# A sparse attention and FFN kernel: the first batch's steps in a written order on all engines, with the first two weight conversions between them

## Chip, core and metric

The kernel runs on one core of one Trainium2 chip. The metric is the device time of one execution in microseconds (us).

## The reference

For each of 8 batches and 8 heads (S = 576 tokens, D = 64) attention runs under a mask: heads 0 to 3 see the last 32 tokens, heads 4 to 7 see earlier tokens of the same class modulo 32. The heads of a token, side by side, are a row of 512 numbers, and 4608 such rows go through a feed-forward layer with 2048 inner units.

```python
scores = scale * np.matmul(q, k.transpose(0, 1, 3, 2))
...
mask_local = (rel >= 0) & (rel < stride)
mask_strided = (rel >= 0) & (pos[None, :] % stride == pos[:, None] % stride)
...
attn = np.exp(scores)
attn = attn / (np.sum(attn, axis=-1, keepdims=True) + 1e-09)
...
h = x @ w_in
g = np.where(pos, h, np.where(neg, 0.0, (h + beta) ** 2 / (4.0 * beta)))
return (g @ w_out).astype(np.float32)
```

## The kernel before

**Engines.** PE multiplies, DVE is VectorE, ACT ScalarE, POOL GpSimd; loads go out on SP's queue. A scheduler places the instructions of all engines but PE by priority; those that pass `tc.keep_in_program_order` keep the order in which they are written. PE's order is the program's.

**Weights.** `w_in` and `w_out` come as 64-bit numbers, cut into 16 pieces `f` of 128 inner units. `load_w` (L141) brings both parts of a piece into a tile `raw_f` of 1 MB; `convert_w` (L160) turns it into `w_f`, a high and a low half in `fp32r`. For each of the two parts (`i` = 0 is `w_in`, 1 is `w_out`): two scalings on ACT (L168, L170), an and/or on DVE (L171), a shift on DVE (L173), an addition on POOL (L174), then the cast to the high half on ACT (L178) and the subtraction that leaves the low half on DVE (L179). `prepare(n)` (L189) converts up to piece `n`, `stage(n)` (L183) issues loads.

**Attention of a batch** (L232) has four units `u`, 0 and 1 for the local heads, 2 and 3 for the strided ones. `score` (L237) multiplies q and k into PSUM, takes the minimum with the mask (DVE, L267), the maximum (L268), subtracts it (POOL, L269), exponentiates (ACT, L270), sums (L271 to L273) and normalises (L275). `flip` (L278) transposes on PE (tile `tp`) and copies to `pT` on ACT (L287); there are two `pT` buffers. `value` (L290) multiplies with `v` into `xp` and splits the result into a high half `xTh` (ACT, L314) and a low half `xTl` (DVE, L315). PSUM has three places "o", two "h" and three "a".

**FFN.** Tokens go in chunks, the first of 512. For each chunk `c` and piece `f`, `up(c, f)` (L332) does 12 matmuls, on three products of halves, and the nonlinearity: `u` on ACT (L345, L346), `h` on DVE (L347), `gh` on ACT (L348), `gl` on DVE (L349). `down` (L352) follows two pieces later. During chunk 0 the second batch's attention is placed between the pieces by `GROUPS` (L386).

**The start** (L368 to L382) is what the change rewrites: the loads of the first batch, then its steps in an order of names, with `prepare(1)` after the second flip and `prepare(3)` behind all:

```python
for g in ("s0", "s1", "s2", "s3", "f0", "f1", "v0", "v1", "f2", "f3", "v2", "v3"):
    first[g]()
    if g == "s3":
        stage(6)
    if g == "f1":
        prepare(1)
```

Of the kernel before, what the change touches and what calls it, by code (L numbers as in the profile page):

```python
# [16 lines left out]
P = 128  # L17
# [6 lines left out]
def tile_sparse_attention_then_ffn(  # L24
# [115 lines left out]

    def load_w(f):  # L141
        at = waits_in(f)
        held.add(at)
        if at < NF:
            raw = place(at, [P, 2, DM, 2], U32, f"raw_{f}")
            raws[f] = [(i, raw[:, i], slice(0, DM)) for i in range(2)]
            tc.keep_in_program_order(nc.sync.dma_start(raw, w_v[f]))

    def pieces(f):
# [4 lines left out]
        for i in range(2):  # L154
            for e in (slice(0, n), slice(n, DM)):
                r = o_p.tile([P, n, 2], U32, tag="ob", name=f"raw_{f}_{i}_{e.start}")
                tc.keep_in_program_order(nc.sync.dma_start(r, w_v[f][:, i, e]))
                yield i, r, e

    def convert_w(f):  # L160

        held.discard(waits_in(f))
        sums = []
        for i, raw, e in pieces(f):
            L, H_ = raw[:, :, 0], raw[:, :, 1]
            t = H_.bitcast(F32)

            tc.keep_in_program_order(nc.scalar.activation(t, t, AF.Copy, scale=2.0 ** -112))  # L168

            tc.keep_in_program_order(nc.scalar.activation(L, L, AF.Copy, scale=2.0 ** -29))  # L170
            tc.keep_in_program_order(nc.vector.scalar_tensor_tensor(  # L171
                out=L, in0=H_, scalar=0x80000000, in1=L, op0=ALU.bitwise_and, op1=ALU.bitwise_or))
            nc.vector.tensor_scalar(out=H_, in0=H_, scalar1=3, scalar2=None, op0=ALU.logical_shift_left)  # L173
            nc.gpsimd.tensor_tensor(out=H_, in0=H_, in1=L, op=ALU.add)  # L174
            sums.append((i, t, e))
        wt[f] = w = place(f, [P, 2, 2, DM], F32R, f"w_{f}")
        for i, t, e in sums:
            nc.scalar.copy(w[:, 0, i, e], t)  # L178
            nc.vector.tensor_tensor(out=w[:, 1, i, e], in0=t, in1=w[:, 0, i, e].bitcast(F32), op=ALU.subtract)  # L179
# [9 lines left out]
    def prepare(n):  # L189
        nonlocal ready  # L190
        while ready < min(NF, n):
            convert_w(ready)
# [6 lines left out]
    def load_qk(b, p):  # L199
# [6 lines left out]
        if b < 2:  # L206
            tc.keep_in_program_order(load)
        loaded[b, p, "qk"] = t

    def load_v(b, p):  # L210
# [3 lines left out]
        if b < 2:  # L214
            tc.keep_in_program_order(load)
# [16 lines left out]
    def attention(b, kinds):  # L232
# [4 lines left out]
        def score(u):  # L237
# [4 lines left out]
            for s in range(n):  # L242
                for p in range(2):
                    for i in range(I):
# [14 lines left out]
            st = st_p.tile([P, 3, 2 * SLOTS * 2], F32, tag="st", name=f"st_{b}_{u}")[:, :, :N]  # L259
# [17 lines left out]

        def flip(u):  # L278
# [3 lines left out]
            for j in range(2):  # L282
# [4 lines left out]
                nc.scalar.copy(pT[:, j, :n], tp)  # L287
            flipped[u] = pT

        def value(u):  # L290
# [6 lines left out]
            for n, R in enumerate(rows):  # L297
# [7 lines left out]
                at += R  # L305
            for p in range(2):
# [7 lines left out]
                nc.scalar.copy(dst[0], src)  # L314
                nc.vector.tensor_tensor(out=dst[1], in0=src, in1=dst[0].bitcast(F32), op=ALU.subtract)  # L315

        return {
            "s0": lambda: score(0),
            "s1": lambda: (score(1), fetch_qk(b, 2)),
            "s2": lambda: score(2),  # L320
            "s3": lambda: (score(3), fetch_qk(b + 1, 0)),
            "f0": lambda: flip(0), "f1": lambda: flip(1), "f2": lambda: flip(2), "f3": lambda: flip(3),
            "v0": lambda: value(0),
            "v1": lambda: (value(1), fetch_v(b + 1, 0)),
            "v2": lambda: value(2),
            "v3": lambda: (value(3), fetch_v(b + 1, 1)),
        }
# [133 lines left out]
```

## Time and profile before

| | us |
|---|---|
| median of 3 runs | 949.81 (949.51 to 950.14) |
| the profiled execution | 950.17 |
| its span, first to last instruction | 948.4 |
| PE busy (8112 matmul records) | 913.5 (96%) |
| weight loads on PE | 802.6 (85%) |
| DVE / ACT / POOL busy | 398.9 / 444.5 / 129.7 |

The profiled execution's own time is 1.8 us over its span. Most matmuls here leave two records in the trace. Busy time of PE counts a matmul at the clock that it had. In the text `x0` stands for the split of unit 0's values (two casts, two subtractions), `f0` for its transposes, `v0` for its value matmuls, and so on.

### The profile page before, as it was taken

To read this page: it belongs to the slowest core of one execution; us is meant where nothing else is said; L and a number is where in the kernel's file an instruction comes from. 1 tells how busy PE (TensorE), PEld (TensorE's weight loads), DVE (VectorE), ACT (ScalarE), POOL (GpSimd) and SP (SyncE) were. 2 spreads that over 40 slices of the span, in tenths; PEclk is the share of its full clock that TensorE was granted. 3 is DMA by queue.
4 is the path that set the end of the run, shared out by engine and by line. 5 is a ranking of instruction groups with operands and counts; after the bars stand their busy time and mean duration, and the time that the engine had idled before them with its cause. 6 is when DMAs were issued, how large, how long until landed. Compare 5 with 4: busy or idle time off the path is not lost.

```text
span 948.4 us, 18897 instructions
## 1 busy us (share of the span) xinstructions
PE 913.5 (96%) x8112; PEld 802.6 (85%) x8112; DVE 398.9 (42%) x744; ACT 444.5 (47%) x875; POOL 129.7 (14%) x135
## 2 busy tenths in 40 slices
PE   4768999999999999999999999999999999999998
PEld 3556788998888889888888888988888888998997
DVE  5798883224445332225434432224343533222221
ACT  3667885334455444434444344334443544433433
POOL 5255430002203100002102100001110210000000
PEclk9979999999999999999999999999999999999999
DMA  9812601002302300002202111002020200000000
GB/s 374 358 80 94 262 32 56 1 1 87 102 33 76 101 32 34 1 1 87 102 31 87 50 53 65 1 1 84 4 101 32 87 1 1 34 1 1 34 1 34
DMA packets 14915, 61.95 MB, mean 65 GB/s; under 512 B 1648, under 2 KB 1648, under 8 KB 11888
## 3 DMA queue, kind: packets, MB, share of 16 engines
q1 hardware_dynamic: 14832, 60.76, 17.7%
q8 instruction: 63, 1.03, 0.5%
q14 instruction: 20, 0.16, 0.1%
HBM read 51.31 MB, written 9.44 MB: 64 GB/s over the span
## 4 chain that ended last, share of the span: by engine, by line
PE 89%; DVE 5%; ACT 3%; POOL 2%; issue 1%; DMA 0%; SPq 0%; POOLq 0%; DVEq 0%
PE o L358 42%; PE h L338 40%; PE xp L303 3%; PE sc L251 2%; PE tp L286 2%; DVE raw L171 1%; POOL raw L174 1%; POOL pr L269 1%; DVE w L179 1%; DVE raw L173 1%; ACT raw L170 1%; ACT raw L168 1%; DVE st L271 0%; ACT pr L270 0%; DMA qk<-in_qk_l 0%
## 5 line engine op out<-in xcount | busy, mean ns | idle before, releaser
L338 PE MATMUL h<-xTh,w 128*128 128x384 f32 (+2 forms) x1536 | 424.8, 339 | 9.4 <-ACT w L178 6.2
L358 PE MATMUL o<-w,gh 128*128 128x512 f32 x1152 | 370.7, 403 | 0.0
L338 PEld LDWEIGHTS h<-xTh,w 128*128 128x128 f32 x1536 | 281.4, 189 | 25.1 <-ACT w L178 6.5
L347 DVE SCALAR_TENSOR_TENSOR h<-h,u 128x384 f32<-128x384 f32 (+2 forms) x192 | 108.5, 565 | 400.8 <-ACT u L346 400.7
L338 PE MATMUL h<-xTl,w 128*128 128x384 f32 (+2 forms) x768 | 260.3, 339 | 0.0
L345 ACT ACTIVATE u<-h,half 128x384 f32<-128x384 f32 (+2 forms) x192 | 111.4, 580 | 309.2 <-PE h L338 306.9
L358 PEld LDWEIGHTS o<-w,gh 128*128 128x128 f32 x1152 | 209.3, 189 | 39.7
L358 PE MATMUL o<-w,gl 128*128 128x512 f32 x576 | 228.7, 397 | 0.0
L338 PEld LDWEIGHTS h<-xTl,w 128*128 128x128 f32 x768 | 145.2, 189 | 10.2
L349 DVE TENSOR_TENSOR gl<-h,gh 128x384 fp32r<-128x384 f32 (+2 forms) x192 | 106.3, 553 | 73.5 <-ACT gh L348 73.3
L348 ACT CAST gh<-h 128x384 fp32r<-128x384 f32 (+2 forms) x192 | 92.6, 482 | 91.6 <-DVE h L347 91.2
L358 PEld LDWEIGHTS o<-w,gl 128*128 128x128 f32 x576 | 108.6, 189 | 26.1
L269 POOL TENSOR_TENSOR pr<-pr,st 128x648 f32<-128x648 f32 (+2 forms) x32 | 41.4, 1296 | 517.3 <-DVE st L268 490.2
L346 ACT ACTIVATE u<-u 128x384 f32<-128x384 f32 (+2 forms) x192 | 101.0, 526 | 5.0
L270 ACT ACTIVATE pr<-pr 128x648 f32<-128x648 f32 (+2 forms) x32 | 23.7, 741 | 63.8 <-POOL pr L269 63.8
L174 POOL TENSOR_TENSOR raw<-raw 128x512 uint32<-128x512 uint32 (+1 forms) x34 | 41.3, 1214 | 61.4 <-DVE raw L173 50.7
L271 DVE TENSOR_REDUCE st<-pr 128x12 f32<-128x648 f32 (+2 forms) x32 | 26.3, 821 | 47.3 <-ACT pr L270 47.3
L275 POOL TENSOR_TENSOR pr<-pr,st 128x648 f32<-128x648 f32 (+2 forms) x30 | 39.7, 1324 | 42.0 <-DVE st L273 41.3
L303 PEld LDWEIGHTS xp<-pT,v 64*64 64x64 f32 (+2 forms) x1856 | 32.6, 143 | 15.1 <-issue 7.7
L303 PE MATMUL xp<-pT,v 64*64 64x32 f32 (+2 forms) x1856 | 36.5, 228 | 7.1 <-DVE xTl L315 4.6
L251 PEld LDWEIGHTS sc<-qk 64*32 64x32 f32 (+1 forms) x2048 | 28.1, 123 | 15.5 <-issue 8.0
L251 PE MATMUL sc<-qk 64*32 64x64 f32 (+1 forms) x2048 | 33.2, 234 | 7.6 <-DMA qk<-in_qk_l 5.3
(33 smaller groups left out, 384.2 us busy)
## 6 DMA issues: line engine op xcount, KB each, us to landing
raw<-in_w SPq DMA_DIRECT2D x15, 1024.0 KB, 11.6
qk<-in_qk_s SPq DMA_DIRECT2D x16, 604.0 KB, 5.7
qk<-in_qk_l SPq DMA_DIRECT2D x16, 576.0 KB, 5.0
v<-in_v_l SPq DMA_DIRECT2D x8, 1152.0 KB, 5.8
out<-ob SPq DMA_DIRECT2D x36, 256.0 KB, 4.0
v<-in_v_s SPq DMA_DIRECT2D x8, 704.0 KB, 4.0
raw<-in_w SPq DMA_DIRECT2D x4, 256.0 KB, 8.5
```

The costliest lines, as they stand in the source:

```text
L174: nc.gpsimd.tensor_tensor(out=H_, in0=H_, in1=L, op=ALU.add)
L251: nc.tensor.matmul(sc[j][i * Q:(i + 1) * Q, s, p], qk[:, 0, q0:q0 + Q], qk[:, 1, k0:k0 + W], start=True, stop=True)
L269: nc.gpsimd.tensor_tensor(out=pr, in0=pr, in1=st[:, 0].unsqueeze(2).broadcast_to([P, N, W]), op=ALU.add)
L275: eng.tensor_tensor(out=pr, in0=pr, in1=st[:, 2].unsqueeze(2).broadcast_to([P, N, W]), op=ALU.mult)
L303: nc.tensor.matmul(xp[p][j * D:(j + 1) * D, at:at + R], loaded[b, p0 // 2, "v"][half_, b0 + n, j], pT[half_, j, s, i * Q:i * Q + R], start ...
L338: nc.tensor.matmul(hp, wt[f][:, x, 0, cc * P:(cc + 1) * P], xT[y][:, cc, r0:r0 + n_t], start=n == 0, stop=n == 3 * NC - 1)
L345: nc.scalar.activation(u, hp, AF.Relu, bias=half, scale=0.5)
L346: nc.scalar.activation(u, u, AF.Square)
L347: nc.vector.scalar_tensor_tensor(out=hp, in0=hp, scalar=1.0, in1=u, op0=ALU.max, op1=ALU.min)
L348: nc.scalar.copy(gh, hp)
L349: nc.vector.tensor_tensor(out=gl, in0=hp, in1=gh.bitcast(F32), op=ALU.subtract)
L358: nc.tensor.matmul(o_ps[c][t], gs[x][:, t * P:(t + 1) * P], wt[f][:, y, 1, :], start=f == 0 and n == 0, stop=f == NF - 1 and n == 2)
```

## The change

`score` is cut into `score`, `soften` and `norm`, `value` into `value` and `split`; in the first batch (`b == 0`) every step of them on ACT, DVE and POOL is kept in the written order, and all four scores come first, then four exponentials, then four normalisations, now all on POOL. `convert_w` becomes a generator of three parts, scalings, bit operations and final split, so that the conversions of `w_0` and `w_1` are placed between the first batch's steps. The low half of `w_0` is subtracted on POOL. The load of `raw_0` goes ahead of `v`, that of `raw_2` ahead of the second batch's `qk`. `st` has four buffers, and the PSUM places of the first batch are written out.

```diff
     def convert_w(f):
...
-        for i, raw, e in pieces(f):
...
+        parts = list(pieces(f))
+        for _, raw, _ in parts:
+            t = raw[:, :, 1].bitcast(F32)
+
+            pin(nc.scalar.activation(t, t, AF.Copy, scale=2.0 ** -112))
+
+            pin(nc.scalar.activation(raw[:, :, 0], raw[:, :, 0], AF.Copy, scale=2.0 ** -29))
+        yield
+        for _, raw, _ in parts:
             L, H_ = raw[:, :, 0], raw[:, :, 1]
...
+            pin(nc.vector.scalar_tensor_tensor(out=L, in0=H_, scalar=0x80000000, in1=L,
+                                               op0=ALU.bitwise_and, op1=ALU.bitwise_or))
+            tie(nc.vector.tensor_scalar(out=H_, in0=H_, scalar1=3, scalar2=None, op0=ALU.logical_shift_left), f < 2)
+            tie(nc.gpsimd.tensor_tensor(out=H_, in0=H_, in1=L, op=ALU.add), f < 2)
+        yield
         wt[f] = w = place(f, [P, 2, 2, DM], F32R, f"w_{f}")
...
+            tie(nc.scalar.copy(w[:, 0, i, e], t), f < 2)
+            eng = nc.gpsimd if f == 0 else nc.vector
+            tie(eng.tensor_tensor(out=w[:, 1, i, e], in0=t, in1=w[:, 0, i, e].bitcast(F32), op=ALU.subtract), f < 2)
...
-            st = st_p.tile([P, 3, 2 * SLOTS * 2], F32, tag="st", name=f"st_{b}_{u}")[:, :, :N]
+            st = st_p.tile([P, 3, 2 * SLOTS * 2], F32, tag="st", bufs=4, name=f"st_{b}_{u}")[:, :, :N]
...
-            eng = nc.vector if b == 0 and u % 2 else nc.gpsimd
-            eng.tensor_tensor(out=pr, in0=pr, in1=st[:, 2].unsqueeze(2).broadcast_to([P, N, W]), op=ALU.mult)
...
+            tie(nc.gpsimd.tensor_tensor(out=pr, in0=pr, in1=st[:, 2].unsqueeze(2).broadcast_to([P, N, W]),
+                                        op=ALU.mult), b == 0)
...
-    FREE = {"s0": "oo", "s1": "aa", "s2": "hh", "s3": "oa", "f0": "oo", "f1": "hh", "f2": "oo", "f3": "hh"}
-    first = attention(0, lambda u, kind, n: FREE.get(kind.lower() + str(u), "aa")[n])
+    FREE = {"s0": "oo", "s1": "aa", "s2": "hh", "s3": "oa", "f0": "oo", "f1": "hh", "f2": "oa", "f3": "oo",
+            "v0": "aa", "v1": "hh", "v2": "oa", "v3": "aa"}
+    first = attention(0, lambda u, kind, n: FREE[kind.lower() + str(u)][n])
...
+            stage(1)
             load_v(0, 0)
             load_v(0, 1)
-            stage(2)
-            for g in ("s0", "s1", "s2", "s3", "f0", "f1", "v0", "v1", "f2", "f3", "v2", "v3"):
-                first[g]()
-                if g == "s3":
-                    stage(6)
-                if g == "f1":
-                    prepare(1)
+            stage(3)
+            w0, w1 = convert_w(0), convert_w(1)
+            first("s0", "s1", "s2", "s3", "e0", "e1", "e2", "e3", "n0", "n1", "n2", "n3")
+            stage(6)
+            next(w0)
+            first("f0", "f1", "f2")
+            next(w0)
+            next(w1)
+            first("v0", "x0")
+            next(w0, None)
+            first("f3")
+            next(w1)
+            first("v1", "x1", "v2", "x2", "v3", "x3")
+            next(w1, None)
+            ready = 2
         prepare(AHEAD)
```

The order that results, at three places. Names read tile, batch, unit or piece, with a running number last; lines are those of each kernel's own text, so L287 before is L312 after, L168/L170 are L173/L175, L171/L173 are L180/L182, L178/L179 are L188/L190, L349 is L378.

ACT, first batch. Before:

```order
L270 ACTIVATE pr_0_3_334<-pr_0_3_334 128x12x54
L314 CAST xTh_144<-xp_0_0_0_393 128x384
L314 CAST xTh_144<-xp_0_0_1_394 128x384
L178 CAST w_0_388<-raw_0_160 128x512 x2
L314 CAST xTh_144<-xp_0_1_0_447 128x192
L314 CAST xTh_144<-xp_0_1_1_448 128x192
L287 COPY pT_0_2_479<-tp_0_2_0_480 128x384
L287 COPY pT_0_2_479<-tp_0_2_1_485 128x384
L287 COPY pT_0_3_490<-tp_0_3_0_491 128x384
L287 COPY pT_0_3_490<-tp_0_3_1_496 128x384
```

ACT, first batch, with the change:

```order
L312 COPY pT_0_2_382<-tp_0_2_0_383 128x384
L312 COPY pT_0_2_382<-tp_0_2_1_388 128x384
L173 ACTIVATE raw_1_162<-raw_1_162 128x512
L175 ACTIVATE raw_1_162<-raw_1_162 128x512
L173 ACTIVATE raw_1_162<-raw_1_162 128x512
L175 ACTIVATE raw_1_162<-raw_1_162 128x512
L344 CAST xTh_144<-xp_0_0_0_403 128x384
L344 CAST xTh_144<-xp_0_0_1_404 128x384
L188 CAST w_0_457<-raw_0_156 128x512 x2
L312 COPY pT_0_3_462<-tp_0_3_0_463 128x384
L312 COPY pT_0_3_462<-tp_0_3_1_468 128x384
```

Unit 2's copies moved ahead of unit 0's casts, and `raw_1`'s scalings came between the two.

DVE, second batch's softmax and the next weights. Before:

```order
L171 SCALAR_TENSOR_TENSOR raw_3_352<-raw_3_352 128x512
L349 TENSOR_TENSOR gl_0_1_709<-h_0_1_694,gh_0_1_708 128x512
L179 TENSOR_TENSOR w_2_584<-raw_2_350,w_2_584 128x512
L173 TENSOR_SCALAR raw_3_352<-raw_3_352 128x512
L171 SCALAR_TENSOR_TENSOR raw_3_352<-raw_3_352 128x512
L179 TENSOR_TENSOR w_2_584<-raw_2_350,w_2_584 128x512
L271 TENSOR_REDUCE st_1_1_750<-pr_1_1_749 128x8
L173 TENSOR_SCALAR raw_3_352<-raw_3_352 128x512
L272 TENSOR_SCALAR st_1_1_750<-st_1_1_750 128x8
L273 RECIPROCAL st_1_1_750<-st_1_1_750 128x8
L179 TENSOR_TENSOR w_3_681<-raw_3_352,w_3_681 128x512
L171 SCALAR_TENSOR_TENSOR raw_4_354<-raw_4_354 128x512
```

DVE, the same place with the change:

```order
L378 TENSOR_TENSOR gl_0_1_709<-h_0_1_694,gh_0_1_708 128x512
L182 TENSOR_SCALAR raw_3_352<-raw_3_352 128x512
L180 SCALAR_TENSOR_TENSOR raw_3_352<-raw_3_352 128x512
L296 TENSOR_REDUCE st_1_1_754<-pr_1_1_753 128x8
L182 TENSOR_SCALAR raw_3_352<-raw_3_352 128x512
L297 TENSOR_SCALAR st_1_1_754<-st_1_1_754 128x8
L298 RECIPROCAL st_1_1_754<-st_1_1_754 128x8
L180 SCALAR_TENSOR_TENSOR raw_4_354<-raw_4_354 128x512
L182 TENSOR_SCALAR raw_4_354<-raw_4_354 128x512
L180 SCALAR_TENSOR_TENSOR raw_4_354<-raw_4_354 128x512
L376 SCALAR_TENSOR_TENSOR h_0_2_779<-h_0_2_779,u_0_2_792 128x512
L190 TENSOR_TENSOR w_3_681<-raw_3_352,w_3_681 128x512
```

The subtractions of `w_2` have moved up, to just before and after the minima of the second batch's unit 0; `w_3`'s first now follows three operations on `raw_4` and one `h`.

ACT, pieces 7 to 9. Before:

```order
L348 CAST gh_0_5_996<-h_0_5_982 128x512
L178 CAST w_7_975<-raw_7_688 128x512 x2
L345 ACTIVATE u_0_6_1099<-h_0_6_1086,half_96 128x512
L178 CAST w_8_1079<-raw_8_690 128x512
L287 COPY pT_1_1_1107<-tp_1_1_0_1108 128x256
L287 COPY pT_1_1_1107<-tp_1_1_1_1112 128x256
L168 ACTIVATE raw_9_692<-raw_9_692 128x512
```

ACT, pieces 7 to 9, with the change:

```order
L377 CAST gh_0_5_996<-h_0_5_982 128x512
L188 CAST w_7_975<-raw_7_688 128x512
L188 CAST w_8_1079<-raw_8_690 128x512 x2
L374 ACTIVATE u_0_6_1099<-h_0_6_1086,half_96 128x512
L312 COPY pT_1_1_1107<-tp_1_1_0_1108 128x256
L312 COPY pT_1_1_1107<-tp_1_1_1_1112 128x256
L173 ACTIVATE raw_9_692<-raw_9_692 128x512
```

Both casts of `w_8` now stand ahead of `u_0_6`; one stood behind the scalings of `raw_9`.

## Rows read from the trace of the kernel before

**Rows 1.** The page's part 2: busy tenths of two engines in 40 slices of 23.7 us.

```profile
PE   4768999999999999999999999999999999999998
...
DVE  5798883224445332225434432224343533222221
```

**Rows 2.** Stretches: length, busy us of PE, PEld, DVE, ACT, POOL, granted clock, DMA share, GB/s.

```profile
35.45:40.00 4.55, 4.55 (x18) 3.25 (x15) 3.46 (x6) 3.28 (x6) 1.10 (x1) 0.62 0.74 257
52.00:60.00 8.00, 5.32 (x12) 3.73 (x13) 7.93 (x14) 4.04 (x7) 5.14 (x4) 0.50 0.02 8
62.00:64.00 2.00, 2.00 (x10) 1.61 (x9) 1.97 (x4) 0.19 (x1) 1.22 (x1) 1.00 0.04 8
156.00:948.40 792.40, 788.81 (x6712) 703.21 (x6710) 275.30 (x543) 339.26 (x682) 62.98 (x60) 1.00 0.12 42
```

**Rows 3.** Timeline of PE, 0 to 60 us: start, length, work, idle before and releaser.

```profile
12.57 1.12 PE L251 MATMUL sc<-qk 64*64 64x54 f32 x33 [1.23 <-issue]
...
18.70 2.56 PE L303 MATMUL xp<-pT,v 64*64 64x32 f32 x84
23.81 0.65 PE L303 MATMUL xp<-pT,v 64*64 64x32 f32 x16 [2.55 <-issue]
...
44.91 0.86 PE L251 MATMUL sc<-qk 64*32 64x64 f32 x64
51.95 0.80 PE L338 MATMUL h<-xTh,w 128*128 128x512 f32 x1 [6.18 <-ACT w L178]
...
55.86 1.22 PE L338 MATMUL h<-xTh,w 128*128 128x512 f32 x2 [2.68 <-DVE w L179]
```

**Rows 4.** Groups by line, 7 to 36 us: count, busy us, mean ns, idle before.

```profile
L287 ACT COPY pT<-tp 128x384 f32<-128x384 f32 x6 | 2.8, 477 | 0.9 <-PE tp L286 0.7
...
L271 DVE TENSOR_REDUCE st<-pr 128x12 f32<-128x648 f32 x2 | 1.6, 819 | 1.9 <-ACT pr L270 1.9
...
L275 POOL TENSOR_TENSOR pr<-pr,st 128x768 f32<-128x768 f32 x1 | 1.5, 1472 | 1.5 <-DVE st L273 1.5
...
L275 POOL TENSOR_TENSOR pr<-pr,st 128x648 f32<-128x648 f32 x1 | 1.3, 1272 | 0.0
...
L269 POOL TENSOR_TENSOR pr<-pr,st 128x512 f32<-128x512 f32 x1 | 1.0, 1038 | 0.0
```

**Rows 5.** Timeline of DVE, POOL, ACT, 35 to 61 us.

```profile
36.16 1.19 DVE L315 TENSOR_TENSOR xTl<-xp,xTh 128x252 fp32r<-128x252 f32 x2 [0.84 <-ACT xTh L314]
...
43.01 0.68 DVE L179 TENSOR_TENSOR w<-raw,w 128x512 fp32r<-128x512 f32 x1
...
56.66 1.53 DVE L179 TENSOR_TENSOR w<-raw,w 128x512 fp32r<-128x512 f32 x1
...
59.35 1.43 DVE L179 TENSOR_TENSOR w<-raw,w 128x512 fp32r<-128x512 f32 x1
...
56.22 1.42 POOL L174 TENSOR_TENSOR raw<-raw 128x512 uint32<-128x512 uint32 x1 [0.97 <-DVE raw L173]
...
53.94 0.67 ACT L168 ACTIVATE raw<-raw 128x512 f32<-128x512 f32 x1
...
55.62 0.68 ACT L170 ACTIVATE raw<-raw 128x512 uint32<-128x512 uint32 x1
```

**Rows 6.** Timeline of PE, 60 to 130 us.

```profile
63.55 0.62 PE L338 MATMUL h<-xTh,w 128*128 128x512 f32 x2
...
65.86 0.82 PE L286 MATMUL tp<-ident,pr 128*128 128x128 f32 x6
...
88.32 0.41 PE L286 MATMUL tp<-ident,pr 128*128 128x128 f32 x2 [2.22 <-DVE xTl L315]
...
110.67 0.85 PE L286 MATMUL tp<-ident,pr 128*128 128x128 f32 x6 [2.18 <-POOL raw L174]
```

**Rows 7.** A stretch with the transfers' rate last, columns as in rows 2.

```profile
32.00:34.00 2.00, 1.31 (x52) 1.18 (x48) 0.02 (x1) 1.11 (x3) 0.00 (x0) 1.00 0.94 386
```

**Rows 8.** The first batch's two `v` transfers: issue to landing.

```profile
DMA to landing us min/median/max: 10.3/10.9/11.5
```

More of the change, by code (lines that the diff above doesn't have):

```diff
@@ L139, in waits_in, with tie @@
         return PLACES[f]
+    pin = tc.keep_in_program_order
+    def tie(ins, when):
+        if when:
+            pin(ins)
     def load_w(f):
@@ L146, in load_w @@
             raws[f] = [(i, raw[:, i], slice(0, DM)) for i in range(2)]
-            tc.keep_in_program_order(nc.sync.dma_start(raw, w_v[f]))
+            pin(nc.sync.dma_start(raw, w_v[f]))
     def pieces(f):
@@ L191, in prepare @@
         while ready < min(NF, n):
-            convert_w(ready)
+            for _ in convert_w(ready):
+                pass
             ready += 1
@@ L206, in load_qk @@
         if b < 2:
-            tc.keep_in_program_order(load)
+            pin(load)
         loaded[b, p, "qk"] = t
@@ L214, in load_v @@
         if b < 2:
-            tc.keep_in_program_order(load)
+            pin(load)
         loaded[b, p, "v"] = t
@@ L305, in value, with split @@
                 at += R
+            flipped[u] = xp, at
+        def split(u):
+            local, b0, _ = UNITS[u]
+            xp, at = flipped.pop(u)
             for p in range(2):
@@ L313, in value, with go @@
                     dst = [t[:, 2 + p, base:base + S].rearrange("p (a r) -> p r a", r=ST)[:, r0:r0 + nr] for t in xT]
[L314 to L327, printed above, removed]
+                tie(nc.scalar.copy(dst[0], src), b == 0)
+                tie(nc.vector.tensor_tensor(out=dst[1], in0=src, in1=dst[0].bitcast(F32), op=ALU.subtract), b == 0)
+        steps = {"s": score, "e": soften, "n": norm, "f": flip, "v": value, "x": split}
+        after = {"s1": lambda: fetch_qk(b, 2), "s3": lambda: fetch_qk(b + 1, 0),
+                 "v1": lambda: fetch_v(b + 1, 0), "v3": lambda: fetch_v(b + 1, 1)}
+        def go(*names):
+            for name in names:
+                steps[name[0]](int(name[1]))
+                after.get(name, int)()
+        return go
     o_ps = {}
@@ L391, in tile_sparse_attention_then_ffn @@
             b = need[c + 1] if c + 1 < len(CHUNKS) and need[c + 1] > need[c] else None
-            groups = attention(b, lambda u, kind, n: "a") if b is not None else {}
+            if b is not None:
+                go = attention(b, lambda u, kind, n: "a")
             for f in range(NF):
```

49 lines of the change are left out of this document (25 added, 24 removed).

## The prediction

> **What bounds the kernel now.** I read the page's slices first, then stretches, then the timeline. In the slices PE is below 9 tenths only in the first four and the last, so what this change can win lies before 95 us; from 156 us on PE is busy 788.81 of 792.40 us [rows 1, 2]. DVE has 9, 8, 8, 8 tenths from 47 to 142 us: behind the idle PE stands a full DVE [rows 1]. Five things are to be seen in the timeline.
> - The first batch is a chain over four engines; `up` of the first weight starts at 35.45 and ends about 40.0, at a mean clock of 0.62 [rows 2].
> - `up(0, 2)` waits 6.18 us for the ACT cast of `w_2`, does two matmuls, and waits 2.68 us for its DVE subtraction [rows 3]. From 52 to 60 DVE is busy 7.93 of 8.00 us and the granted clock is 0.50, its lower level (1.2 GHz) [rows 2]. At the upper one ten matmuls of 512 columns fit into 2.00 us [rows 2], with starts 0.23 apart; at the lower one I count 0.43.
> - `w_3` is complete at 59.35 + 1.43 = 60.78 and PE reaches its third matmul with it at 63.55: a margin of 2.8 us [rows 5, 6].
> - Later PE waits twice more behind DVE's backlog, 2.22 us before 88.32 and 2.18 before 110.67 [rows 6].
> - PE stops for nothing visible ("issue") 1.23 us before 12.57 and 2.55 before 23.81 [rows 3].
>
> The first part of a weight (`w_in`) is all that `up` needs. The profiled execution took 950.17 us, 0.36 above the median of 949.81; 0.2%, what a measurement can tell, is 1.9 us.
>
> **Step A, the first batch: about 1 us lost.** Scores end as before, at 12.57 + 1.12 = 13.7. Before, unit 0 was summed and normalised before unit 2's scores were touched; now DVE does unit 3's minimum and maximum first and then unit 0's sum, three passes of 0.8 to 0.95 us and two short ones [rows 4], so POOL's first normalisation starts at 16.9. POOL does all four in a row (those of units 1 and 3 were DVE's, which has time to spare here), 1.47 + 1.04 + 1.27 = 3.8 for three [rows 4]: unit 2 is ready at 20.7. Its transposes (1.5) end at 22.4, and `v0`, 96 matmuls at 2.56 / 84 us [rows 3], at 25.4. ACT's copies of unit 2 need a buffer that `v0` still reads (two `pT` buffers, three units flipped), and stand ahead of everything else: copies 1.0 to 26.6, `w_1`'s four scalings 2.36 (53.94 to 56.30 in [rows 5]) to 28.9, `x0` 0.9, `w_0` 1.2, unit 3's copies 1.0: 32. `v3` follows to 32.9, its casts to 34.6. DVE waits for `x0`'s casts until 29.4 and subtracts to 30.4. Then `w_1`'s four raw operations (2 x 1.08), the two `w_0` subtractions now on POOL and one POOL addition (3 x 1.04) exclude each other, to 35.5, and the six subtractions of `x1` to `x3` (1.19 the last two [rows 5]) take 3.1: 38.6, against 36.16 + 1.19 = 37.35 [rows 5]. `up(0, 0)`, again at half clock, runs 35.9 to 41.0, not 40.0: +1.0.
>
> The loads cost nothing: the `v` transfers landed by 3.1 + 11.5 = 14.6 [rows 8], and one of 1 MB ahead of them takes 2.7 us at 386 GB/s [rows 7], 17.3, five before `v0`. `raw_0`, first used near 17.7, goes out two places earlier. `w_2`'s load moves ahead of the second batch's `qk`; neither is used before 36. If that cover were gone, `v0` would slip by what lands late, at most the 2.7. Other PSUM places and a fourth `st` buffer only let four units stand side by side; I cost them at nothing, covered by the same chain.
>
> **Step B, `w_1` and `w_2`: PE gains 11.5 us.** `w_1` is subtracted right after, 39.8. `w_2` now stands ahead of the second batch's softmax on DVE; its raw operations with one addition of POOL between give 44.4. PE is at 41.0 + 1.3 (96 scores, at 0.86 for 64 [rows 3]) + 2.8 (`up(0, 1)`, twelve at 0.23) + 0.86 = 46.0: no wait. `up(0, 2)` ends at 48.8 and `down(0, 0)` at 51.6; before, `down(0, 0)` ended two matmuls ahead of 63.55 [rows 6], at 63.1.
>
> **Step C, `w_3`: all of it given back.** The softmax work that `w_2` overtook now lies between `w_2` and `w_3`, and so do three operations on `raw_4` and one `h` that stood behind `w_3`. From 46.5 (second part of `w_2`) there are 22 DVE operations up to and with `w_3`'s first subtraction: nine of 0.68 [rows 5], three shifts of 0.4, four reductions of 0.67 to 0.95 (0.82 in [rows 4]), a pair of minima of 0.74, four short ones of 0.2: 12 us. To them come 0.6 for the exponential behind POOL, 0.8 for `gh` (it stands behind four scalings on ACT) and 1.7 for POOL. A DVE subtraction beside a POOL addition takes 1.53 and not 0.68 [rows 5]. Sum: 61.6. Without any wait it would be 58.5, with every POOL operation of the stretch in the way 63.5; I take 61.6 since subtractions in [rows 5] that met POOL all paid for it.
> The Trainium skill ("SBUF — State Buffer", Who interferes with whom) has it that a DVE operation with two SBUF inputs and a GpSimd operation that reads SBUF hold one port pair in turn, each for its whole length. By that rule moving two normalisations and two subtractions to POOL is no saving where DVE has work; the rows agree (1.53 against 0.68), and without the rule the sum would be about 59.9.
>
> PE has waited from 51.6, with two matmuls at 58, so its clock will be low, as after the 6.18 us [rows 2, 3]. Ten matmuls at 0.43 from 61.6 end at 65.9; before, that point was 65.86 [rows 6]. The net of A to C is 0.
>
> **Step D, from 66 to 120 us: +0.5.** DVE is 2.6 us ahead here, PE is not. The wait before 88.32 shrinks by 1.0. Then ACT's order costs: the second `w_8` cast, which waits for POOL, now stands ahead of `u_0_6`, and DVE idles 3 us; its lead becomes a lag of 0.7, the transposes at 110.67 come at 110.9, and `w_10`, behind three more operations, makes PE wait 0.3 to 1. I take +0.5. Bounds: -2.6 if the lead holds, +1.5. Behind that PE is the bound, as before. Sum: 950.17 + 0.0 + 0.5 - 0.36 = **950.3**.
>
> **Rivals.**
> - *DVE's waits do not add up* (faster). For it: 12 of the 15.1 us of step C are work, the rest are waits that overlap one another; DVE leads by 2.6 afterwards. Against: DVE was busy 7.93 of 8.00 us with the same kind of work [rows 2]. `w_3` at 58.5 and half-clock matmuls end at 62.8, 3.1 early: 947.2; with the lead of step D kept too, 944.6. It decides from `w_3` before 60.
> - *PE's instructions come late in `v3`* (slower). The two "issue" stops lie 33 + 6 + 4 + 84 = 127 matmul records apart, the 10 transposes between them left out [rows 3]. The stretch entered at 12.57 lasted to 21.26, and the next ran only at 23.81, 11.2 us later. In the new order that stop falls inside `v0`, about 24.9, after the time at which it ended before; the next, 128 records on, falls on the ninth matmul of `v3`, 32.2, only 7.3 us later, with transfers still at 386 GB/s [rows 7]. At 11.2 us `v3` is 3.9 late, and with it the last casts, `w_1`, `w_2` and the DVE queue: +3, 953.3. It decides above 7.3 us. The Trainium skill ("Runtime: NRT & Kernel Launch", Instruction fetch mechanics) tells of blocks of 256 instructions whose crossing is "mostly hidden"; by that this rival costs nothing. The trace differs with 1.23 and 2.55 us.
> - *No wait for `w_3`* (much faster): the 11.5 us of step B kept, less 1 to 2 at 88 and 110: 940. It needs a DVE that does 12 us of work in 5; its chance is small and lies in the first rival's.
>
> **How the numbers follow.** Forecast 0.38 (own range 948.4 to 952.2), first rival 0.35 with the third in it, second 0.27 with the upper bounds of C and D. They give faster by over 0.2% 0.35, within 0.38, slower 0.27. The range reaches to both rivals, 944.8 to 954.0, and leaves out the third and a sum of all mishaps.
>
> **What would show it.** Right: no wait of PE for `w_2`; one of 8 to 10 us for `w_3` starting near 52, ended by ACT and then by DVE; half clock to about 66; ACT's copies of unit 2 starting only after `v0`; the transposes of the second batch's unit 2 near 111. Wrong: `w_3` complete before 60, PE's `up` of `w_4` starting before 67, an "issue" stop of over 1 us in `v3`, or `up(0, 0)` ending later than 42.

## The result and the profile after

The changed kernel takes 951.10 us (median of 20 runs, 950.07 to 952.54), the kernel before 949.95 (20 runs, 948.29 to 950.76). The ratio is 1.0015 with a 95% interval of 1.0008 to 1.0021: 1.15 us slower, which lies within the 0.2% that the prediction counted as no change. The profiled execution has a span of 949.6 us, against 948.4 before.

First PE's line of the page's part 2, whose slices answer to [rows 1]:

```profile
PE   4879799999999999999999999999999999999998
```

PE's first five slices had 4, 7, 6, 8 and 9 tenths; they now have 4, 8, 7, 9 and 7. Part of the idle time has moved to the fifth, 95 to 119 us. The timeline of PE from 12 to 70 us, which answers to [rows 3] (start, length, work, idle time before it and what ended it):

```profile
12.85 1.12 PE L263 MATMUL sc<-qk 64*64 64x54 f32 x33 [1.23 <-issue]
19.10 2.56 PE L311 MATMUL tp<-ident,pr 128*128 128x128 f32 x10 [5.13 <-POOL pr L299]
...
32.03 1.67 PE L328 MATMUL xp<-pT,v 54*64 54x54 f32 x40 [1.29 <-ACT pT L312]
36.40 0.79 PE L367 MATMUL h<-xTh,w 128*128 128x512 f32 x1 [2.69 <-DVE xTl L345]
...
41.81 1.40 PE L263 MATMUL sc<-qk 64*32 64x64 f32 x96
...
47.56 0.50 PE L367 MATMUL h<-xTh,w 128*128 128x512 f32 x1 [0.61 <-DVE gl L378]
...
53.00 0.39 PE L387 MATMUL o<-w,gl 128*128 128x512 f32 x1
58.09 0.80 PE L367 MATMUL h<-xTh,w 128*128 128x512 f32 x1 [4.70 <-DVE raw L180]
...
61.38 1.22 PE L367 MATMUL h<-xTh,w 128*128 128x512 f32 x2 [2.07 <-DVE w L190]
...
65.81 1.11 PE L311 MATMUL tp<-ident,pr 128*128 128x128 f32 x6
```

`up(0, 0)` starts at 36.40 and not at 35.45. The wait of 6.18 us for `w_2` is gone; 0.61 is left, for `gl`, the last step of the nonlinearity of `up(0, 0)`, which frees the PSUM bank that `up(0, 2)` writes. `down(0, 0)` ends at 53.4, where it ended at 63.1. Then come 4.70 and 2.07 us for `w_3`, with two matmuls between them, and ten matmuls at the lower clock (1.2 GHz; their starts are 0.43 apart). The row puts the 4.70 down to a step on `raw_4` that ended as PE started; what PE needs there is `w_3`'s first cast on ScalarE, which stands behind four scalings:

```profile
57.31 1.27 ACT L188 CAST w<-raw 128x512 fp32r<-128x512 f32 x2
```

In run 6 below the same wait is put down to that cast. The transposes of the second batch's unit 0 start at 65.81; before, at 65.86 [rows 6]. Of 9.7 us in hand at 53, nothing is left at 66. What PE lost to the change lies later, in the timeline from 103 to 125 us, of the changed kernel and then of the kernel before:

```profile
109.37 0.85 PE L311 MATMUL tp<-ident,pr 128*128 128x128 f32 x6 [1.82 <-DVE xTl L345]
...
116.41 0.50 PE L367 MATMUL h<-xTh,w 128*128 128x512 f32 x1 [3.39 <-DVE gl L378]
...
117.72 1.05 PE L367 MATMUL h<-xTh,w 128*128 128x512 f32 x2
...
120.84 0.97 PE L328 MATMUL xp<-pT,v 54*64 54x54 f32 x48
...
132.95 0.82 PE L311 MATMUL tp<-ident,pr 128*128 128x128 f32 x6
```

```profile
118.55 0.92 PE L303 MATMUL xp<-pT,v 54*64 54x54 f32 x48
...
130.64 0.82 PE L286 MATMUL tp<-ident,pr 128*128 128x128 f32 x6
```

PE comes to the transposes of unit 2 at 109.37, which is 1.3 us earlier than in [rows 6], and then waits 3.39 us ahead of `up(0, 10)` for `gl`, the last step of piece 8's nonlinearity on VectorE. `up(0, 10)` then runs partly at the lower clock (two matmuls take 1.05 us, not 0.62; a mean grant of 0.66 from 116 to 121 us, the row below with columns as in [rows 2]). The step behind it starts at 120.84 and not at 118.55, and unit 3's transposes are 132.95 - 130.64 = 2.3 us late.

```profile
116.00:121.00 5.00, 4.59 (x18) 3.19 (x20) 3.44 (x6) 3.45 (x7) 0.00 (x0) 0.66 0.00 0
```

VectorE and ScalarE show why; first VectorE, then ScalarE, 104 to 117 us:

```profile
112.45 0.68 DVE L376 SCALAR_TENSOR_TENSOR h<-h,u 128x512 f32<-128x512 f32 x1
...
113.63 2.12 DVE L190 TENSOR_TENSOR w<-raw,w 128x512 fp32r<-128x512 f32 x2
115.67 0.68 DVE L378 TENSOR_TENSOR gl<-h,gh 128x512 fp32r<-128x512 f32 x1
```

```profile
104.97 0.66 ACT L173 ACTIVATE raw<-raw 128x512 f32<-128x512 f32 x1
...
106.63 0.70 ACT L175 ACTIVATE raw<-raw 128x512 uint32<-128x512 uint32 x1
107.20 0.71 ACT L374 ACTIVATE u<-h,half 128x512 f32<-128x512 f32 x1
```

Piece 8's first step `u` (107.20) stands behind four scalings of `raw_10` on ScalarE. Its `h` on VectorE follows at 112.45, and its `gl`, behind both subtractions of `w_10`, at 115.67. There are two `h` banks in PSUM, so `up(0, 10)` can't write before that `gl` has read the one it gets.

The span is only 1.2 us longer, so 1.1 us came back after 133 us, where PE hardly waits. The last transposes of the program start at 791.02, before at 789.53: PE took 658.07 us from unit 3's transposes to there, against 658.89, over the same matmuls. That is 0.8 of the 1.1. The prediction had nothing for it; the fifth run and the last two are about it.

### The profile page after: what moved, and what is told of

It reads as the page before. It is cut to its first block, busy times and chain, and to the rows that moved or that the text cites. A ratio compares the mean times of both kernels' runs of the same rounds, so it can differ in the third digit from the quotient of the medians.

```text
span 949.6 us, 18899 instructions
## 1 busy us (share of the span) xinstructions
PE 914.8 (96%) x8112; PEld 801.7 (84%) x8112; DVE 399.5 (42%) x740; ACT 444.5 (47%) x875; POOL 135.5 (14%) x139
## 2 busy tenths in 40 slices
DMA packets 14915, 61.95 MB, mean 65 GB/s; under 512 B 1648, under 2 KB 1648, under 8 KB 11888
## 3 DMA queue, kind: packets, MB, share of 16 engines
q1 hardware_dynamic: 14832, 60.76, 17.9%
## 4 chain that ended last, share of the span: by engine, by line
PE 89%; DVE 6%; ACT 2%; POOL 1%; issue 1%; DMA 1%; SPq 0%; POOLq 0%; ACTq 0%; DVEq 0%
PE o L387 41%; PE h L367 40%; PE xp L328 3%; PE sc L263 3%; PE tp L311 2%; DVE raw L180 1%; DVE raw L182 1%; DMA qk<-in_qk_s 1%; DVE w L190 1%; POOL pr L287 1%; ACT raw L173 0%; DVE xTl L345 0%; DVE gl L378 0%; DVE h L376 0%; DVE st L296 0%
## 5 line engine op out<-in xcount | busy, mean ns | idle before, releaser
L378 DVE TENSOR_TENSOR gl<-h,gh 128x384 fp32r<-128x384 f32 (+2 forms) x192 | 106.5, 555 | 74.7 <-ACT gh L377 74.5
L287 POOL TENSOR_TENSOR pr<-pr,st 128x648 f32<-128x648 f32 (+2 forms) x32 | 41.3, 1291 | 513.9 <-DVE st L286 491.4
L289 ACT ACTIVATE pr<-pr 128x648 f32<-128x648 f32 (+2 forms) x32 | 23.7, 742 | 65.5 <-POOL pr L287 65.5
L299 POOL TENSOR_TENSOR pr<-pr,st 128x648 f32<-128x648 f32 (+2 forms) x32 | 42.1, 1315 | 43.2 <-DVE st L298 42.4
```

Of the source, the lines that this page charges most:

```text
L287: tie(nc.gpsimd.tensor_tensor(out=pr, in0=pr, in1=st[:, 0].unsqueeze(2).broadcast_to([P, N, W]), op=ALU.add), b == 0)
L299: tie(nc.gpsimd.tensor_tensor(out=pr, in0=pr, in1=st[:, 2].unsqueeze(2).broadcast_to([P, N, W]), op=ALU.mult), b == 0)
L378: nc.vector.tensor_tensor(out=gl, in0=hp, in1=gh.bitcast(F32), op=ALU.subtract)
```

## Experiments

All are timed in five rounds beside the kernel before. "up(0, 0)" and "tp" are the times in each run's own trace, of one execution, at which that step and the first transposes of the second batch start. Before, run 5 and run 11 have the same order in the first batch and differ by 0.6 us at up(0, 0), so less than that is not read as an effect.

| run | time, us | ratio to before (95%) | up(0, 0) | tp |
|---|---|---|---|---|
| before | 949.95 | | 35.45 | 65.86 |
| the change | 951.10 | 1.0015 (1.0008 to 1.0021) | 36.40 | 65.81 |
| 1 piece 8's nonlinearity first | 948.76 | 0.9988 (0.9979 to 0.9997) | 36.67 | 66.07 |
| 2 `w_3` first | 948.55 | 0.9986 (0.9977 to 0.9995) | 36.38 | 59.39 |
| 3 `w_1` behind the batch | 944.15 | 0.9939 (0.9926 to 0.9951) | 32.32 | 61.35 |
| 4 `w_1`'s scalings in the gap | 948.67 | 0.9985 (0.9976 to 0.9994) | 34.49 | 63.19 |
| 5 before, four `st` buffers | 948.88 | 0.9991 (0.9982 to 0.9999) | 35.64 | 66.17 |
| 6 `w_1`'s raw work in the gap | 946.93 | 0.9971 (0.9960 to 0.9983) | 31.73 | 60.76 |
| 7 run 3, engines back | 946.13 | 0.9963 (0.9949 to 0.9976) | 33.26 | 63.06 |
| 8 run 3, loads back | 943.97 | 0.9944 (0.9932 to 0.9957) | 32.60 | 61.95 |
| 9 runs 1 and 6 | 944.04 | 0.9940 (0.9926 to 0.9953) | 32.00 | 61.09 |
| 10 runs 1, 2 and 6 | 941.40 | 0.9912 (0.9899 to 0.9926) | 31.93 | 54.99 |
| 11 before, padded | 943.99 | 0.9933 (0.9919 to 0.9947) | 36.06 | 66.64 |
| 12 run 10, padded | 936.21 | 0.9855 (0.9838 to 0.9871) | 31.99 | 55.12 |

**Run 1: does piece 8's nonlinearity (the expectations call it GELU) hold `up(0, 10)`?** `marks` keeps instructions by name: `u`, `h`, `gl` of `up(c, f)`; of piece f, half i, ScalarE's scalings `a` and `b`, VectorE's first two operations `o` and `sh`, GpSimd's addition `ad`, the subtraction `l`; `mn` and `mx` of a unit's softmax and GpSimd's addition in it, `pa`. `chain` makes them issue in that order.

```diff
+    def chain(*keys):
+        info = mybir.DependencyInfo(mybir.DependencyClass.NoSync, mybir.DependencyReason.DATA)
+        for early, late in zip(keys, keys[1:]):
+            tc.add_manual_dep(marks[late].ins, marks[early].ins.name, info, reason="chain")
...
         for a in pend:
             down(*a)
+        chain(('u', 0, 8), ('a', 10, 0))
+        chain(('gl', 0, 8), ('l', 10, 0))
```

> The changed kernel with two orders set: on ScalarE the first step of piece 8's GELU (u) ahead of w_10's scalings, on VectorE its last (gl) ahead of w_10's subtractions. Theory: PE's 3.39 us before up(0, 10) and the low clock after it (1.6 us) come from this gl, which frees the PSUM bank that up(0, 10) writes. Then the wait there falls below 1 us, up(0, 10) runs at the full clock, and the time is 2.3 us under the changed kernel's 951.1: 948.8 (948.2 to 949.6). Rival: VectorE's backlog is the limit whatever the order, and PE waits as long for w_10 or w_11 instead: 950.6 to 951.5.

948.76, 2.3 us under the change, as the theory had it. PE's timeline, 103 to 125 us:

```profile
110.70 1.23 PE L321 MATMUL tp<-ident,pr 128*128 128x128 f32 x6 [2.89 <-POOL raw L193]
...
115.95 0.39 PE L377 MATMUL h<-xTh,w 128*128 128x512 f32 x1
...
118.77 0.92 PE L338 MATMUL xp<-pT,v 54*64 54x54 f32 x48
```

`up(0, 10)` starts without a wait and at the full clock. The wait before the transposes has grown by 1.07 us (2.89, from 1.82) and the lower clock lies behind it, so the rival has a part; the step behind `up(0, 10)` is at 118.77, 2.1 us earlier than in the change.

**Run 2: is the wait for `w_3` order or work?** `w_3`'s first two operations are also freed from their place behind the second batch's softmax.

```diff
+        chain(('b', 2, 1), ('a', 3, 0), ('b', 3, 0), ('a', 3, 1), ('b', 3, 1), ('u', 0, 0))
+        chain(('l', 2, 1), ('o', 3, 0), ('o', 3, 1), ('sh', 3, 0), ('sh', 3, 1), ('gl', 0, 0), ('mx', 1, 0), ('h', 0, 1), ('l', 3, 0),
+              ('mn', 1, 1, 0), ('mn', 1, 1, 1), ('gl', 0, 1), ('l', 3, 1), ('mx', 1, 1), ('o', 4, 0))
+        chain(('ad', 3, 0), ('ad', 3, 1), ('pa', 1, 0))
```

> The changed kernel with w_3's conversion ahead of the second batch's unit 1 and of raw_4 on VectorE, its scalings ahead of piece 0's GELU on ScalarE, its additions ahead of the second batch's softmax on GpSimd. Theory: the wait for w_3 (4.70 + 2.07 us and half clock to 66) is a matter of order; it falls below 1 us, PE reaches the transposes of the second batch's unit 0 near 57 and not 65.81, and though they and w_4 then wait, at least 3 us are kept: 948 or less. Rival: VectorE has too much work up to there whatever the order, the wait moves to those transposes or to w_4, and the time stays within 1 us of 951.1.

948.55: between the two. PE's timeline:

```profile
49.40 0.50 PE L377 MATMUL h<-xTh,w 128*128 128x512 f32 x1 [3.29 <-DVE gl L388]
...
59.39 0.82 PE L321 MATMUL tp<-ident,pr 128*128 128x128 f32 x6
...
66.08 0.50 PE L377 MATMUL h<-xTh,w 128*128 128x512 f32 x1 [3.07 <-ACT w L198]
...
113.41 0.50 PE L377 MATMUL h<-xTh,w 128*128 128x512 f32 x1 [3.39 <-DVE gl L388]
```

PE no longer waits for `w_3`; it waits 3.29 us for `gl` ahead of `up(0, 2)` instead, and the transposes come at 59.39, 6.4 us earlier. 3.07 us go back ahead of `up(0, 4)`, whose weight is now the late one, and at `up(0, 10)`, with its 3.39 us unchanged, PE is 3.0 us ahead. Order made the wait at that place. Part of the gain goes back at the next weight; whether another order there would keep it was not tried.

**Run 3: what is the early `w_1` worth?**

```diff
-            w0, w1 = convert_w(0), convert_w(1)
+            w0 = convert_w(0)
...
-            next(w1)
...
-            next(w1)
...
-            next(w1, None)
-            ready = 2
+            ready = 1
```

(and `f < 2` becomes `f < 1` where the written order is kept.)

> The changed kernel without w_1 among the first batch's steps (its conversion stands behind them, as before the change). Theory: what the early w_1 and w_2 win up to 53 us is given back at w_3, so that without it PE waits in up(0, 1) and up(0, 2), but not for w_3: the second batch's first transposes within 2 us of 65.8 and the time within 1.5 us of 951.1. Rival: the early w_1 is worth something at the end too: 953 or more.

944.15. Both were wrong: without the early `w_1` the kernel is 6.95 us faster than the change. PE's timeline:

```profile
32.32 0.79 PE L367 MATMUL h<-xTh,w 128*128 128x512 f32 x1
...
49.38 0.80 PE L367 MATMUL h<-xTh,w 128*128 128x512 f32 x1 [6.72 <-ACT w L188]
...
51.87 1.22 PE L367 MATMUL h<-xTh,w 128*128 128x512 f32 x2 [1.27 <-DVE w L190]
...
61.35 0.82 PE L311 MATMUL tp<-ident,pr 128*128 128x128 f32 x6
```

`up(0, 0)` starts 4.1 us earlier, and the wait for `w_2` is back, 6.72 and 1.27 us, about as long as that for `w_3` in the change (4.70 and 2.07). So the lead stays: the transposes come 65.81 - 61.35 = 4.5 us earlier. The scheduler's order behind has changed too, PE does not wait at `up(0, 10)`, and at unit 3's transposes, which start at 125.67, the lead is 7.3 us. So the early `w_1` gave PE 9.7 us that this order did not keep, and took 4.1 us from the first batch that it did not win back. The other 2.8 of the 7.3 us arise behind the transposes, with the changed order.

**Run 4: where do the 4.1 us come from?** ScalarE waits for `v0` before it can copy unit 2, with `w_1`'s scalings behind it:

```profile
26.67 0.86 ACT L312 COPY pT<-tp 128x384 f32<-128x384 f32 x2 [4.59 <-PE xp L328]
27.41 0.68 ACT L173 ACTIVATE raw<-raw 128x512 f32<-128x512 f32 x1
...
29.64 0.85 ACT L344 CAST xTh<-xp 128x384 fp32r<-128x384 f32 x2
```

```diff
-            first("f0", "f1", "f2")
+            first("f0", "f1")
             next(w0)
             next(w1)
+            first("f2")
             first("v0", "x0")
```

> The changed kernel with ScalarE's four scalings of w_1 ahead of its copies of unit 2's probabilities, in the 4.59 us in which it waits for v0 to free a pT buffer. Nothing else moves. Theory: ScalarE's later work of the first batch comes 2.3 us earlier, up(0, 0) at 34.2 to 35 and not 36.40, and since VectorE's queue from there on is what w_3 waits for, w_3 and the end come 1.5 to 2.3 us earlier: 949.2. Rival: the early part is covered by what holds w_3, and the time stays within 0.5 us of 951.1.

948.67, 2.4 us under the change: the theory, and slightly more than it gave. `up(0, 0)` starts at 34.49, 1.9 us earlier; the transposes come at 63.19, 2.6 us earlier, and the end keeps it. ScalarE's order is nearly half of the 4.1.

**Run 5: the 1.1 us behind 133 us.** In the kernel before:

```diff
-    st_p = ctx.enter_context(tc.tile_pool(name="st_p", bufs=3))
+    st_p = ctx.enter_context(tc.tile_pool(name="st_p", bufs=4))
```

> The kernel before with the changed kernel's four st buffers and nothing else; every order stays, the tiles allocated behind st move by 288 bytes per partition. From the third transposes of unit 3 of the second batch to the last ones PE needs 658.89 us before and 658.07 to 658.08 in the changed kernel and all four variants of it run so far, over the same instructions. Theory: the difference comes with the moved tiles, so this kernel needs 658.1 as well and its time is 1.1 under the kernel before: 948.8 to 949.2. Rival: it comes from elsewhere (the first batch's places, code layout), and the time is that of before within 0.4 us.

948.88. PE's timeline has unit 3's transposes at 130.70 and the last ones at 788.77: 658.07 us, as in the changed kernel. The expectation had the shift wrong: an `st` buffer takes 160 bytes per partition, so `u`, `gh`, `gl` and the output buffers moved by 160 and not by 288.

**Run 6: the rest of the 4.1 us.** From the change:

```diff
-            first("f0", "f1", "f2")
+            first("f0", "f1")
             next(w0)
             next(w1)
+            next(w1)
+            first("f2")
             first("v0", "x0")
             next(w0, None)
             first("f3")
-            next(w1)
```

> The changed kernel with w_1's scalings on ScalarE ahead of unit 2's copies (as in the run with that order alone) and also w_1's four raw operations on VectorE and two additions on GpSimd ahead of x0 and of w_0's subtractions, in the time in which both wait for v0. Theory: w_1 was dear because it stood on the first batch's path, not because it came early; in the gap it costs that path under 1 us, up(0, 0) starts by 33.3, VectorE takes up w_2 some 2 us before the run without an early w_1, and the time is under that run's 944.15: 941 to 943.5. Rival: VectorE and GpSimd hinder each other there, x0's subtractions come late, up(0, 0) starts at 34 or later and the time is 944.5 to 948.

946.93. The first half of the theory held: `up(0, 0)` starts at 31.73, as early as in run 3 or earlier, because `w_1`'s raw operations now fill the time in which VectorE waited for `v0`. The time was missed, by 3.4 us. PE's timeline:

```profile
52.99 0.80 PE L367 MATMUL h<-xTh,w 128*128 128x512 f32 x1 [4.61 <-ACT w L188]
...
60.76 1.48 PE L311 MATMUL tp<-ident,pr 128*128 128x128 f32 x6
...
111.55 0.79 PE L367 MATMUL h<-xTh,w 128*128 128x512 f32 x1 [3.39 <-DVE gl L378]
```

VectorE's order behind the batch is that of the change, so PE has its waits too: 4.61 us for `w_3`, and 3.39 at `up(0, 10)`, whose cost the sum had left out.

**Run 7: the moves to GpSimd.** In run 3's kernel:

```diff
+            eng = nc.vector if b == 0 and u % 2 else nc.gpsimd
-            tie(nc.gpsimd.tensor_tensor(out=pr, ...
+            tie(eng.tensor_tensor(out=pr, ...
...
-            eng = nc.gpsimd if f == 0 else nc.vector
+            eng = nc.vector
```

> The run without an early w_1 (944.15), with the normalisations of units 1 and 3 and w_0's two subtractions back on VectorE. Theory (the prediction's): VectorE has time to spare there and holds the same port when it does them, so the move to GpSimd neither saves nor costs: 943.6 to 945.2, up(0, 0) within 0.7 us of 32.32. Rival: the move is what makes the first batch shorter: 946.5 or more.

946.13, 2.0 us over run 3 and between the two; the theory's 0.7 us for `up(0, 0)` is missed as well. `up(0, 0)` starts at 33.26, 0.9 us later, but 0.71 of that is a stop of "issue" within `v3`, which run 3 does not have:

```profile
32.15 1.18 PE L329 MATMUL xp<-pT,v 54*64 54x54 f32 x34 [0.71 <-issue]
```

Run 8, with the moves as in the change, has one of 0.37 us at the same place, so it is not shown to come from the moves; without it 0.2 us are left. The rest arises behind `up(0, 0)`, where the order on VectorE changed as well. What the moves to GpSimd are worth stays open.

**Run 8: the loads.** In run 3's kernel:

```diff
-            stage(1)
             load_v(0, 0)
             load_v(0, 1)
-            stage(3)
+            stage(2)
```

> The run without an early w_1 (944.15), with the loads in the order of before (v ahead of raw_0, w_2's load behind the second batch's qk). Theory (the prediction's): the loads are hidden either way: 943.6 to 944.7. Rival: raw_0 then lands after 18 us, w_0's scalings on ScalarE wait for it with all that stands behind them, and the time is 945.5 or more.

943.97, 0.2 us from run 3: the loads are hidden. (The trace is of an execution of 945.51 us, the longest of the five.)

**Runs 9 and 10: do the orders add up?** Run 9 is run 6's edit with run 1's two chains, run 10 has run 2's edit too.

> The run with w_1 in the gap (946.93) and the two orders for piece 8's GELU of the first run. Theory: that run kept the wait of 3.39 us and the low clock at up(0, 10), which took back what its earlier start won; the orders are worth the 2.3 us that they were worth on the changed kernel: 944.6 (944.0 to 945.3). Rival: with PE earlier by 4 us, VectorE is the limit there and the wait moves to the transposes or to w_11: 946 or more.

944.04: run 1's order is worth 2.9 us here; the theory had 2.3 and a range of 944.0 to 945.3.

> The same, and w_3 ahead of the second batch's unit 1 as in the second run. Theory: the three orders add up, since they act in three places: 944.6 less the 2.5 of the second run: 942.1 (941 to 943.5), PE at the second batch's first transposes before 57. Rival: VectorE's work alone sets when w_5 to w_11 are ready, PE only waits later, and the time is that without this order, 944 to 945.5.

941.40: another 2.6 us. PE's timeline:

```profile
54.99 0.82 PE L321 MATMUL tp<-ident,pr 128*128 128x128 f32 x6
...
61.90 0.79 PE L377 MATMUL h<-xTh,w 128*128 128x512 f32 x1 [3.29 <-ACT w L198]
```

The transposes come at 54.99, 10.8 us earlier than in the change. The wait ahead of `up(0, 4)` (3.29 us) is now the longest behind them.

**Runs 11 and 12: the addresses.** In the kernel before:

```diff
+    pad_p = ctx.enter_context(tc.tile_pool(name="pad_p", bufs=1))
+    nc_pad = pad_p.tile([P, 72], F32, name="pad")
+    tc.nc.vector.memset(nc_pad, 0.0)
```

> The kernel before with three st buffers as it has, and a tile of 288 bytes per partition behind them that nothing reads (one memset at the start). Theory: what the fourth st buffer brought is the moved addresses of the tiles behind it (GELU results and output buffers, which PE and ScalarE read in the steady state): 658.1 us again between the two sets of transposes, and a time of 948.7 to 949.2. Rival: it is the fourth buffer itself, a softmax that waits less: 658.9 us and the time of before, 949.6 to 950.2.

943.99: 6.0 us under before, which neither had foreseen. Up to 130 us little changed (unit 3's transposes are at 130.22, before at 130.64); from there to the last ones PE takes 654.55 us (784.77 less 130.22), 4.3 less than before. Of two forms of matmul between 350 and 420 us, one of `up` and the one of `down` that loads `gl` as weights (count, busy us, mean ns), in the kernel before, then in this run:

```profile
L338 PE MATMUL h<-xTh,w 128*128 128x384 f32 x131 | 36.2, 337 | 0.0
...
L358 PE MATMUL o<-w,gl 128*128 128x512 f32 x51 | 20.2, 397 | 0.0
```

```profile
L341 PE MATMUL h<-xTh,w 128*128 128x384 f32 x136 | 37.7, 337 | 0.0
...
L361 PE MATMUL o<-w,gl 128*128 128x512 f32 x51 | 19.8, 388 | 0.0
```

`up`, which reads none of the moved tiles, takes as long as before; `down`, which reads `gh` and `gl`, is what became faster.

Run 12 adds a pad to run 10 that nothing writes or reads, so that only addresses differ:

```diff
+    pad_p = ctx.enter_context(tc.tile_pool(name="pad_p", bufs=1))
+    pad_p.tile([P, 32], F32, name="pad")
```

> The run with all three orders (941.4), with a tile of 128 bytes per partition behind st that no instruction touches: every instruction and every order as in that run, and u, gh, gl and the output buffers at the addresses that they have in the run with the pad (160 bytes from the fourth st buffer and these 128). Theory: the pad's 6.0 us came from these addresses alone; beside the 1.1 of the fourth st buffer that leaves 4.9: 936.5 (936.0 to 937.2), and 654.5 to 654.6 us between the two sets of transposes, against 658.07. Rival: it came from the pad's memset, which shifts VectorE's start and its instruction stream: 941.4 and 658.07.

936.21, with unit 3's transposes and the last ones in the timeline of PE at

```profile
122.53 0.82 PE L323 MATMUL tp<-ident,pr 128*128 128x128 f32 x6
```

```profile
777.03 0.82 PE L323 MATMUL tp<-ident,pr 128*128 128x128 f32 x6
```

which is 654.50 us. ScalarE, VectorE and GpSimd do the same operations in the same order as in run 10; the addresses alone did it. This is the fastest version: 1.45% under the kernel before (0.9855, 0.9838 to 0.9871).

## Why the prediction was right, and where it was not

- **The forecast** was 950.3, "no change"; the time is 951.10, inside its own range of 948.4 to 952.2. The mechanism was right up to 66 us. Two terms behind that were wrong with opposite signs: +2.3 where +0.5 stood, and -1.1 where nothing stood. That they nearly cancel is luck: without the -1.1 the time would be about 952.2, the upper end of that range.
- **Step A** said that `up(0, 0)` ends at 41.0; it ended at 41.9, +1.9 and not +1.0. The term that was mis-sized is "POOL does all four in a row": it starts at 17.57 and not at 16.9, and GpSimd waits 0.4 us between each two for VectorE's short operations. The timeline of GpSimd and then that of VectorE:

```profile
17.57 1.47 POOL L299 TENSOR_TENSOR pr<-pr,st 128x768 f32<-128x768 f32 x1 [0.44 <-DVE st L298]
19.45 1.04 POOL L299 TENSOR_TENSOR pr<-pr,st 128x512 f32<-128x512 f32 x1 [0.41 <-DVE st L298]
20.93 1.27 POOL L299 TENSOR_TENSOR pr<-pr,st 128x648 f32<-128x648 f32 x1 [0.44 <-DVE st L298]
```

```profile
18.00 1.06 DVE L297 TENSOR_SCALAR st<-st 128x8 f32<-128x8 f32 x1
...
21.50 0.72 DVE L297 TENSOR_SCALAR st<-st 128x12 f32<-128x12 f32 x1
```

  These additions of a constant to 12 or 8 numbers took 1.06 and 0.72 us beside GpSimd, and each ended 0.02 us after GpSimd's operation; later, alone, one takes 0.17:

```profile
51.88 0.17 DVE L297 TENSOR_SCALAR st<-st 128x12 f32<-128x12 f32 x1
```

  Unit 2 was ready at 22.2, not 20.7. Of these 1.5 us 0.5 reach `up(0, 0)`, which starts at 36.4 and not at 35.9; it then takes 5.5 us where the sum had 5.1. That ScalarE's copies of unit 2 wait for `v0`, with `w_1` behind them, was right (4.59 us, above), and run 4 shows what it costs: 2.4 us.
- **What step A did not ask** was what the order is worth without `w_1`. Run 3 answers: the written order starts `up(0, 0)` at 32.32, 3.1 us earlier than before, and the early `w_1` turns that into 0.95 later. The prediction booked the early `w_1` as a gain (step B) and its price only within the sum of A.
- **The moves to POOL** were priced as no saving, by [rows 5] and by the Trainium skill ("SBUF — State Buffer", Who interferes with whom: each of the two holds the shared port pair for its whole instruction). The trace agrees that the two hinder each other: one and/or of `raw_1` on VectorE, at 33.11, takes 1.79 us beside GpSimd's subtractions of `w_0`, where the other, begun just before them, takes 0.68. Run 7 doesn't refute the price: with the moves undone `up(0, 0)` starts 0.9 us later, but 0.7 of that is the stop in `v3`, and the 2.0 us by which the run is longer are not shown to be the moves'.
- **The loads** at nothing: right (run 8, 0.2 us). **The `st` buffer** at nothing: wrong, and not for a reason in the first batch. It moved other tiles, 1.1 us (run 5).
- **Step B** said no wait for `w_2` and 11.5 us in hand. There was none for `w_2`, but 0.61 us for `gl`, and 9.7 us were in hand. 0.9 of the difference is A's.
- **Step C** said that `w_3`'s first subtraction ends at 61.6, that PE does two matmuls at 58 and that ten at the lower clock end at 65.9. It was

```profile
60.40 0.92 DVE L190 TENSOR_TENSOR w<-raw,w 128x512 fp32r<-128x512 f32 x1
```

  that is 61.3, with the two matmuls at 58.09 and the transposes at 65.81. Counting the operations that stand ahead on VectorE and pricing each with what it meets on GpSimd was the step that carried the forecast; of its waits, those for the exponential and for `gh` came with 0.55 and 0.76 us where 0.6 and 0.8 stood. The first rival (`w_3` before 60) fell. What the sum took for given is that the order is what it is: run 2 shows that another one reaches the transposes at 59.39.
- **Step D** said +0.5 and was +2.3 at 133 us. VectorE's idle time of "3 us" for `u_0_6` came (2.87), but its lead did not turn into a lag; the transposes were at 109.37 and not 110.9. The step that failed is "`w_10`, behind three more operations, makes PE wait 0.3 to 1": the place was right, but what came late was the `gl` that frees the bank, 3.39 us, and with it the lower clock in `up(0, 10)`. The working followed the weights in VectorE's queue and not the operations that free PSUM.
- **The second rival**, a stop of "issue" in `v0` or `v3`, fell by its size: the change has only the 1.23 us before 12.85, and none shows in `v0`. But the place in `v3` was nearly right. The stops in `v3` of runs 7 and 8 (0.71 and 0.37 us) come behind its sixth and seventh record, where the rival had the ninth matmul; they lie 253 and 254 matmul records behind the stop in the scores, where the rival counted 127 and then 128 more. (Matmuls of scores and values leave two records each, the others one.) In the change PE waits 1.29 us for ScalarE just ahead of `v3` (32.03); whether that hides a stop is not shown, nor what stops PE. The Trainium skill's "mostly hidden" ("Runtime: NRT & Kernel Launch", Instruction fetch mechanics) fits these small stops and the change behind 13 us, but not the 1.23 us ahead of 12.85, nor the 2.55 us in [rows 3], which runs 5 and 11 have as well.

## What to carry to other kernels

Work put early is free only if it fills a wait of the engine that does it: the same `w_1` cost 4.1 us of the first batch when it stood on the path, and nothing when it stood in the gap that ScalarE and VectorE had there anyway (`up(0, 0)` at 31.73 in run 6, at 32.32 without it). When a stage waits for a busy engine, count that engine's queue up to the operation that releases, and do it for every release, those that free a buffer too; a gain that only the waiting engine makes ahead of a full queue (9.7 us here) is lost at the next wait unless the order behind it is changed as well, while one that moves the queue itself is kept (run 4, 1.9 us at `up(0, 0)` and 2.4 at the end). And look at what a new buffer moves in memory before putting a percent down to the order.

## What the runs showed of the hardware

PE's speed in a stretch without waits depends on where the tiles `u`, `gh`, `gl` and the output buffers lie in SBUF. Over the same matmuls it took 658.89 us with them as before, 658.07 to 658.11 with them 160 bytes further (the change and runs 1 to 10), and 654.50 to 654.55 with them 288 bytes further (runs 11 and 12), whatever else the kernel did; a matmul on `gl` went from a mean of 397 to 388 ns in one stretch. That is 5.2 us of 941.4 for 128 bytes in run 12. PE reads only `gh` and `gl` of these tiles; which tile matters, and why, stays open: only these three places were tried. On VectorE, operations on a few numbers took up to six times as long beside GpSimd (1.06 us against 0.17), as they ended only with its operation. A chain of such steps that alternates with GpSimd's goes at GpSimd's pace, 0.41 to 0.44 us of gap for each.
